# 163 filling products put in front of 23 operations of the attention, by a table

## The chip, the cores and the metric

The kernel runs on one NeuronCore of one Trainium2 chip. Its engines are TensorE (PE, with its weight loads as PEld), VectorE (DVE), ScalarE (ACT), GpSimd (POOL) and SyncE (SP, which issues DMAs). The metric is the device time of one execution in microseconds; lower is better. Before the change three runs took 992.38, 987.22 and 990.80 us, so the median is 990.8 us.

## The reference

Three layers are computed one after the other. The first is a recurrent attention over 768 steps, for 4 batches and 8 heads of width 40:

```
y[t]  = r[t] . state
Sa    = state . a[t]
state = state * w[t] - outer(Sa, b[t]) + outer(v[t], k[t])
```

The second is a gated MLP on x of 4 x 768 x 320: `h = relu(x @ w_in)`, its second half is normalised and mixed along the sequence by `w_spatial`, and the gated product goes through `w_out`. The third sends every token to one of 8 experts (`relu(x @ w1[e]) @ w2[e]`, scaled by the expert's probability). All three give fp32.

## The kernel before, in words

The attention takes the first 480 us or so and is the only part that the diff touches. The 768 steps are cut into 12 chunks of 64, so that 4 batches give 48 units, numbered q = 0 to 47 in the order of the work; one unit is all 8 heads of one batch and chunk, as 4 pairs of heads. A unit passes through named operations, each a handful of instructions on one engine:

- Preparation, long ahead of use: `loadE` (DMA), `stF` (scans of the decay, DVE), `stK` and `stB` (DVE or POOL), `stQ` (PE, line 280), `stT` (PE, line 298), `stL`, `stLk`, `stKT` (ACT, out of PSUM).
- Inverses of small triangular blocks: groups of units go out to DRAM, are inverted by long rows of small DVE operations (`pm`/`psb` or `cm`/`cs`) and come back by DMA; then for two units at a time `gA`, `pA`, `c1`, `c2` on PE (lines 366, 376 and 379, 391, 399), with copies on DVE and ACT between them.
- The chain from unit to unit: `s` (line 434), `z` (443, with 415 for the next unit), `w` (452, 453), `t` (462) and `y` (470, 471) on PE, with `sc`, `zc`, `wc` on ACT and `tc`, `yc` on DVE between them.

The order of all these on each engine is written out before the program runs, by the function `plan`: a list of operations with durations and due times, run through a small model. Where the model sees PE without work it puts in a filling product: `heat(bank)` multiplies a 128x128 tile of zeros (`hz`) by a 128x256 tile of zeros into a PSUM bank that nobody uses just then (line 229), and the result is never read. A `tied` filling product (line 239) does the same with one operand that DVE has just written, so that it can't run before that DVE operation. A PSUM bank is one of five tiles (`pk`, `pw`, `pq`, `pvr`, `pc`); `takes` says which operation starts to use a bank, `gives` which one reads it out last. A filling product that comes first on a bank gets a new tile there, and waits for the bank's last reader.

The list that `plan` returns is written into the program one by one, by the loop at the end of `attention`; each engine runs its own instructions in that order. In the program a filling product is two instructions, a weight load and a product. An fp32 product of the attention is four in the trace (two weight loads, two products), a transpose (`stT`) two.

## Time and profile before

| | |
|---|---|
| runs, us | 992.38, 987.22, 990.80 (median 990.8) |
| profiled execution, us | 995.05 |
| its span, first to last instruction, us | 993.5 |
| mean granted TensorE clock | 0.938 |
| PE busy, us (share) | 928.7 (93%), 14053 products |
| PE weight loads busy | 820.3 (83%) |
| DVE busy | 687.4 (69%) |
| ACT busy | 549.8 (55%) |
| POOL busy | 385.2 (39%) |
| filling products (line 229) | 607, in the attention alone |

Times in the profile count from the span's start. A busy PE is not a PE at its peak: products overlap, and their ends are modelled. [...] "issue" as the releaser of a wait means that the profile shows nothing that the engine waited for.

### The profile page before, as it was taken

The numbers are of one execution on the slowest core, as the hardware profiler recorded it, in microseconds if no ns is written. First come the engines' busy times: TensorE is split into PE (matmuls) and PEld (weight loads), VectorE is DVE, ScalarE is ACT, GpSimd is POOL, SyncE is SP. The second block draws the span as 40 slices with busy tenths as digits, with TensorE's granted clock in tenths as the row PEclk, the third lists the DMA queues.
The fourth block names the chain that finished last, engine by engine and source line by source line (L and its number), as shares of the span: only waits on it lengthen the run. The fifth ranks groups of instructions, "written<-read, shape, count | busy, mean of one in ns | idle before, by whom it ended". The sixth has DMA issues, their size and how long they took to land. (4 is left out here: it accounts for less than half of the span.)

```text
span 993.5 us, 33733 instructions
## 1 busy us (share of the span) xinstructions
PE 928.7 (93%) x14053; PEld 820.3 (83%) x14053; DVE 687.4 (69%) x1614; ACT 549.8 (55%) x1251; POOL 385.2 (39%) x560
## 2 busy tenths in 40 slices
PE   8879989999899998899899999999999999999995
PEld 6657767787787776787789999999878999999994
DVE  6666779888669888764676464654675777787782
ACT  7766543766546774466344433434343767667671
POOL 6544733745216541452243025050136443333431
PEclk9687997999869999679899999999999999999998
DMA  6665761757615865245320030210147656444640
GB/s 160 169 165 136 166 154 50 190 127 187 164 45 128 214 156 113 67 113 131 112 61 1 10 89 1 56 42 1 50 166 270 257 209 248 167 161 160 266 158 16
DMA packets 172415, 127.52 MB, mean 128 GB/s; under 512 B 127502, under 2 KB 161168, under 8 KB 170593
## 3 DMA queue, kind: packets, MB, share of 16 engines
q1 hardware_dynamic: 166704, 78.06, 30.9%
q0 software_dynamic: 5552, 47.25, 12.6%
q8 instruction: 112, 1.84, 0.8%
q14 instruction: 47, 0.38, 0.1%
HBM read 108.13 MB, written 26.61 MB: 136 GB/s over the span
## 5 line engine op out<-in xcount | busy, mean ns | idle before, releaser
L1242 DVE TENSOR_TENSOR eWL<-raw,eWH 128x1024 fp32r<-128x1024 f32 (+1 forms) x64 | 86.2, 1356 | 21.2 <-ACT eWH L1240 19.9
L1240 ACT CAST eWH<-raw 128x1024 fp32r<-128x1024 f32 (+1 forms) x85 | 94.4, 1140 | 2.2 <-DMA raw<-in_wt_dram,wid 2.2
L1369 POOL DMA_INDIRECT out_dram<-yo,sid x29 | 39.2, 1352 | 111.7 <-ACT yo L1368 44.9
L229 PEld LDWEIGHTS <-hz 128*128 128x128 bf16 x607 | 56.9, 106 | 27.7 <-issue 11.8
L1279 PE MATMUL e_ph<-xh,eWH 128*128 128x256 f32 x288 | 77.9, 284 | 0.0
L294 POOL TENSOR_SCALAR_AFFINE_SELECT lq<-lq 64x256 f32<-64x256 f32 x96 | 47.0, 489 | 78.1 <-ACT lq L290 70.0
L1279 PE MATMUL e_ph<-xl,eWH 128*128 128x256 f32 x288 | 77.0, 280 | 0.0
L1279 PE MATMUL e_py<-eWH,hh 128*128 128x320 f32 x232 | 73.0, 315 | 0.0
L1279 PE MATMUL e_py<-eWH,hl 128*128 128x320 f32 x232 | 72.3, 312 | 0.2 <-DVE hl L1352 0.2
L1279 PE MATMUL e_py<-eWL,hh 128*128 128x320 f32 x232 | 71.5, 308 | 0.0
L936 PE MATMUL pv<-sh,g_vh 128*128 128x384 f32 x192 | 66.4, 346 | 1.3 <-ACT pv L926 1.2
L936 PE MATMUL pv<-sh,g_vl 128*128 128x384 f32 x192 | 64.9, 338 | 1.1 <-POOL g_vl L916 0.6
L273 POOL TENSOR_TENSOR lq<-etile,GP 64x256 f32<-64x256 f32 (+1 forms) x60 | 46.8, 780 | 46.3 <-DVE GP L262 28.5
L936 PE MATMUL pv<-sl,g_vh 128*128 128x384 f32 x192 | 64.6, 336 | 0.0
L426 POOL TENSOR_SCALAR_AFFINE_SELECT X<-X 64x256 f32<-64x256 f32 x48 | 23.2, 483 | 97.3 <-ACT X L422 81.2
L1326 DVE SCALAR_TENSOR_TENSOR hl<-e_ph,hh 128x256 fp32r<-128x256 f32 x96 | 37.9, 418 | 26.3 <-ACT hh L1325 23.3
L470 PE MATMUL py<-X,kt 128*40 128x104 f32 x384 | 51.4, 269 | 4.6 <-DVE X L465 4.3
L465 DVE TENSOR_TENSOR X<-pw,ut 64x416 f32<-64x416 f32 x48 | 27.8, 578 | 40.4 <-PE pw L462 28.8
L1279 PEld LDWEIGHTS e_ph<-xh,eWH 128*128 128x128 f32 x288 | 54.4, 189 | 0.9 <-ACT xh L1269 0.2
L1279 PEld LDWEIGHTS e_ph<-xl,eWH 128*128 128x128 f32 x288 | 54.3, 188 | 0.1
L1325 ACT ACTIVATE hh<-e_ph 128x256 fp32r<-128x256 f32 x96 | 36.5, 384 | 31.0 <-PE e_ph L1279 25.9
L1279 PE MATMUL e_ph<-xh,eWL 128*128 128x256 f32 x192 | 53.6, 279 | 0.0
(363 smaller groups left out, 3159.8 us busy)
## 6 DMA issues: line engine op xcount, KB each, us to landing
etile<-in_ed_dram SPq DMA_DIRECT2D x96, 161.2 KB
DT<-in_dd_dram SPq DMA_DIRECT2D x96, 80.0 KB
pu<-BP SPq DMA_DIRECT2D x48, 128.0 KB
yT<-yt SPq DMA_DIRECT2D x48, 104.0 KB
X<-in_vd_dram SPq DMA_DIRECT2D x96, 50.0 KB
groom<-in_w_dram SPq DMA_DIRECT2D x20, 192.0 KB
xs<-xr SPq DMA_DIRECT2D x3, 1176.0 KB
praw<-in_win_dram SPq DMA_DIRECT2D x6, 512.0 KB
```

The lines of the kernel that those rows point to most:

```text
L229: nc.tensor.matmul(out=hcur[bank],lhsT=hz[:,0:128],rhs=hz,start=True,stop=True)
L273: eng.tensor_tensor(out=LQ[q][r,sl],in0=ar[r],in1=GP[q%NBIG][r,:,0:64],op=ALU.mult)
L294: nc.gpsimd.affine_select(out=LQ[q][r,h],in_=LQ[q][r,h],pattern=[[0,NP],[1,64]],**sel)
L465: nc.vector.tensor_tensor(out=x[0:64,:,0,:],in0=pw[0:64],in1=ut[0:64].unsqueeze(1).to_broadcast([64,NP,104]),op=ALU.mult)
L470: nc.tensor.matmul(out=py[0:40,p,:],lhsT=KT[q][:,p,0:40],rhs=x[:,p,0,:],start=False,**acc)
L936: for j,(l,r) in enumerate(t): nc.tensor.matmul(out=pv,lhsT=l,rhs=r,start=False,stop=j==len(t)-1,skip_group_check=True)
L1240: nc.scalar.copy(WH[:,c0:c1],raw[:,c0:c1])
L1242: else: V.tensor_tensor(out=WL[:,lc(c0):lc(c1)],in0=raw[:,c0:c1],in1=WH[:,c0:c1].bitcast(F32),op=ALU.subtract)
L1279: for i,(l,r) in enumerate(t): nc.tensor.matmul(out=out,lhsT=l,rhs=r,start=i==0,stop=i==len(t)-1)
L1325: nc.scalar.activation(hh[:,j],ph,AF.Relu)
L1326: V.scalar_tensor_tensor(out=hl[:,j],in0=ph,scalar=0.0,in1=hh[:,j].bitcast(F32),op0=ALU.max,op1=ALU.subtract)
L1369: nc.gpsimd.indirect_dma_start(out=out,out_offset=IO(ap=self.sid[:,h,s:s+1],axis=0),in_=yo[:,h],in_offset=None,bounds_check=B*S-1,oob_is_e ...
```

## The change

A table `HEATS` names 23 operations and a count for each, 163 in all. When the loop that writes the planned list into the program comes to one of them, it first writes that many filling products, one after the other, into the first bank of a list `rest`. That list holds the banks which no operation uses at that place of the list; a bank leaves it when an operation takes it, and goes to its end when the operation that reads it out last has been written. So its first member has been free for the longest. `plan` itself knows nothing of the table: the order of all other instructions is as it was, on every engine.

```diff
+HEATS={('s', 2):8,('z', 0):14,('stQ', 5):18,('stQ', 7):6,('stT', 8):3,('stT', 9):5,('stQ', 9):7,('gA', 4):4,('c1', 4):7,('pA', 6):3,('stT', 22):5,('pA', 8):12,('s', 12):3,('stQ', 28):3,('s', 13):9,('y', 15):4,('c1', 20):3,('pA', 22):14,('pA', 36):6,('c1', 36):6,('pA', 38):11,('pA', 42):8,('y', 46):4}
 def plan(ops,K,late,cols,takes,gives):
...
+    rest=["pk","pw","pq","pvr","pc"]
     with tc.manual_schedule():
         for t_,_,n,e in out:
             o=ops.get(n)
             if n[0]=="heat": heat(n[1]); continue
             if n[0]=="tied": tied(n[1],n[2]); continue
-            for k in takes.get(n[0],()): hcur.pop(k,None)
+            if n in HEATS:
+                for _ in range(HEATS[n]): heat(rest[0])
+            for k in takes.get(n[0],()):
+                hcur.pop(k,None)
+                if k in rest: rest.remove(k)
+            if n[0] in gives and gives[n[0]] not in rest: rest.append(gives[n[0]])
```

The table's rows tell a reader little without their places, so here are two of them on PE. The lines below the table are numbered one higher after the change (line 229 becomes 230, and so on). The first place is `pA` of the units 22 and 23, behind `y` of unit 19; in the names `XT` is the inverse, `GA` a tile that DVE wrote just before, `hz` the zeros. Before:

```order
L470 MATMUL py<-X_144,kt 40x104
L471 MATMUL py<-X_144,kt 40x104
L376 MATMUL pc<-XT_146,GA 32x32 x4
L379 MATMUL pc<-GA,XT_146 32x16 x2
L376 MATMUL pc<-XT_146,GA 32x32 x4
```

Between `y` and `pA` stood nothing. After:

```order
L471 MATMUL py<-X_144,kt 40x104
L472 MATMUL py<-X_144,kt 40x104
L230 LDWEIGHTS hz
L230 MATMUL pq<-hz 128x256
...
L230 LDWEIGHTS hz
L230 MATMUL pq<-hz 128x256
L377 MATMUL pc<-XT_146,GA 32x32 x4
L380 MATMUL pc<-GA,XT_146 32x16 x2
L377 MATMUL pc<-XT_146,GA 32x32 x4
```

Fourteen pairs of weight load and product have come in front of `pA` (two of them are shown), on the bank `pq`. Nothing else moved. The second place is `stQ` of unit 28, behind a transpose `stT`; `pq` and `pvr` are its two output banks, `kb` and `lq` its operands. Before:

```order
L399 MATMUL pc<-XT_145,GT_122 32x32 x16
L462 MATMUL pw<-Wt,XT_146 64x104 x8
L298 MATMUL pk<-ident,kb 128x104 x4
L280 MATMUL pq<-lq,kb 64x64 x2
L280 MATMUL pvr<-lq,kb 64x64 x2
```

After:

```order
L463 MATMUL pw<-Wt,XT_146 64x104 x8
L299 MATMUL pk<-ident,kb 128x104 x4
L230 LDWEIGHTS hz
L230 MATMUL pq<-hz 128x256
L230 LDWEIGHTS hz
L230 MATMUL pq<-hz 128x256
L230 LDWEIGHTS hz
L230 MATMUL pq<-hz 128x256
L281 MATMUL pq<-lq,kb 64x64 x2
L281 MATMUL pvr<-lq,kb 64x64 x2
```

Three filling products came in between, on the bank that `stQ` itself takes next; the tile is given up to it.

## Rows read from the trace of the kernel before

**Rows 1.** Windows of three stages; busy us (count) by engine, granted clock, DMA.
```profile
core 0: us, PE busy (x) PEld busy (x) DVE busy (x) ACT busy (x) POOL busy (x), PEclk, DMA share, GB/s
20.00:86.00 66.00, 55.13 (x1043) 41.72 (x1042) 40.85 (x104) 41.77 (x126) 29.80 (x48) 0.74 0.60 161
85.00:476.00 391.00, 363.88 (x9685) 302.52 (x9681) 301.77 (x719) 228.84 (x579) 168.68 (x274) 0.91 0.56 134
476.00:994.00 518.00, 494.58 (x3223) 465.58 (x3223) 332.02 (x756) 263.06 (x505) 171.96 (x212) 0.98 0.33 119
```

**Rows 2.** The page, span and granted clock in 40 slices.
```profile
span 993.5 us, 33733 instructions
PEclk9687997999869999679899999999999999999998
```

**Rows 3.** Windows of stretches at half clock, and one at full.
```profile
149.60:163.30 13.70, 13.70 (x270) 11.10 (x261) 12.70 (x32) 4.97 (x14) 1.20 (x3) 0.50 0.08 21
197.50:200.80 3.30, 3.30 (x52) 2.55 (x51) 2.24 (x2) 0.70 (x2) 1.53 (x3) 0.50 0.90 178
265.70:293.00 27.30, 27.06 (x594) 23.56 (x595) 13.48 (x34) 11.99 (x33) 3.60 (x8) 0.50 0.18 46
398.80:412.50 13.70, 13.70 (x289) 11.82 (x287) 8.03 (x21) 6.54 (x17) 3.77 (x6) 0.50 0.17 42
419.30:432.90 13.60, 13.60 (x327) 12.21 (x327) 9.29 (x25) 7.06 (x14) 2.73 (x5) 0.50 0.41 100
300.00:398.00 98.00, 90.14 (x2528) 74.38 (x2526) 83.28 (x205) 61.25 (x152) 45.01 (x76) 1.00 0.66 154
```

**Rows 4.** Who PE waited for, 85 to 476 us: total, times, longest.
```profile
PE pc L376 <- issue: 7.2, 5, 2.6
PE py L470 <- DVE X L465: 4.3, 4, 2.0
PE pc L391 <- issue: 2.3, 3, 0.8
```

**Rows 5.** Timeline of PE, five waits; in brackets the idle time before.
```profile
149.19 0.18 PE L376 MATMUL pc<-XT,GA 32*32 32x32 f32 x1 [1.40 <-issue]
...
265.94 0.27 PE L376 MATMUL pc<-XT,GA 32*32 32x32 f32 x3 [2.60 <-issue]
...
385.69 0.23 PE L376 MATMUL pc<-XT,GA 32*32 32x32 f32 x4 [1.08 <-issue]
...
397.65 0.22 PE L376 MATMUL pc<-XT,GA 32*32 32x32 f32 x3 [1.57 <-issue]
...
417.87 0.37 PE L470 MATMUL py<-X,kt 128*40 128x104 f32 x2 [2.02 <-DVE X L465]
```

**Rows 6.** Windows from block end to block end; counts of products and weight loads in brackets.
```profile
137.89:140.63 2.74, 2.73 (x127) 2.46 (x126) 2.60 (x8) 1.95 (x7) 1.34 (x2) 1.00 0.70 169
385.68:388.53 2.85, 2.84 (x126) 2.55 (x126) 2.58 (x7) 1.62 (x5) 0.00 (x0) 1.00 0.23 56
145.73:147.60 1.87, 1.87 (x131) 1.70 (x128) 1.80 (x7) 0.28 (x1) 0.00 (x0) 1.00 0.41 79
381.81:384.43 2.62, 2.62 (x149) 2.31 (x138) 2.52 (x8) 1.21 (x3) 0.00 (x0) 1.00 0.77 214
278.47:281.69 3.22, 3.22 (x144) 2.93 (x140) 2.30 (x6) 0.84 (x2) 0.00 (x0) 0.50 0.02 5
```

**Rows 7.** DMA queue, kind: packets, MB, share of 16 engines; whole run.
```profile
q8 instruction: 112, 1.84, 0.8%
```

**Rows 8.** Timeline of PE, early filling products, and waits at 13.65 and 43.34 us.
```profile
5.67 1.89 PE L229 MATMUL pvr<-hz 128*128 128x256 bf16 x8
...
10.55 1.14 PE L229 MATMUL pvr<-hz 128*128 128x256 bf16 x9
13.65 0.29 PE L415 MATMUL pvr<-DT 40*64 40x64 f32 x2 [1.96 <-DMA DT<-in_dd_dram]
...
43.34 0.18 PE L239 MATMUL pc<-GP,hz 104*128 104x32 bf16 x1 [2.25 <-DVE GP L262]
```

## The prediction

> **What bounds the kernel now.** I read the three stages first. From 85 to 476 us PE is busy 363.88 of 391 us and its granted clock is 0.91; before that it is 0.74; behind 476 us, where the change puts nothing, PE is busy 495 of 518 us at 0.98 [rows 1]. So the last stage only moves as a whole: what the attention gains or loses, the kernel gains or loses. The page shows where the clock is low: in slices 2 to 4, 7, 11 to 12 and 17 to 18 of 40 above all [rows 2]. [...]

> Then I compared such stretches with one at full clock. From 300 to 398 us the clock is 1.00 and the fullest engine beside PE is DVE, 83.28 of 98 us or 85%. From 265.7 to 293 us, at 0.50, PE is busy 27.06 of 27.3 us and DVE 13.48, only 49%. From 398.8 to 412.5 us it is 13.70 and 8.03 (59%). There PE alone sets the pace, and it does so since its clock is halved. From 149.6 to 163.3 us PE is full too, but DVE has 12.70 of 13.7 us [rows 3]: there a faster PE would meet a full DVE.

> What PE did just before a fall: it waited. The idle times of 1.40 us up to 149.19, 2.60 up to 265.94 and 1.57 up to 397.65 each have a stretch at 0.50 at their end or within two microseconds of it; the one of 1.08 us up to 385.69 has none. The stretch from 419.3 follows 2.02 us in which `y` waited for DVE [rows 3, 5]. In the waits of `pA` the releaser is "issue": no semaphore explains them.

> [...]

> **The change part by part.** It adds 163 products and 163 weight loads, takes nothing away and moves nothing else. Filling products took 1.89/8 = 0.24 us apiece from 5.67 us on and 1.14/9 = 0.127 from 10.55 on, the tail of the last one included [rows 8]: half pace, then full pace. 163 at full pace are 163 x 0.127 = 20.7 us of PE, the far end of their cost.

> Most of that lies in waits that PE has anyway. The counts fit them: 14 fills (1.8 us) ahead of `pA` of unit 22, inside which 2.60 are waited; 12 (1.5) where 1.40 is waited; 11 (1.4) for 1.57; 6 (0.8) for 1.08 [rows 5]; 18 (2.3) ahead of the 2.25 us up to 43.34; the 8 and 14 of the first units ahead of 1.96 us of waiting for a DMA [rows 8] and of the copies of the next units. No such wait stands behind `stQ` 7 and 28, `s` 13, `y` 15 and `pA` 42: 6+3+9+4+8 = 30 fills, 3.8 us. That is the upper end of what is uncovered; the lower end is nothing, since PE has slack where DVE sets the pace. I take the 12 fills of `y` 15 and `pA` 42, which stand in or near the chain from unit to unit: 1.5 us.

> The bank costs nothing: the first of `rest` has been read out longest ago, and the operation that takes it next stands on PE itself. If one did wait for the last reader once, the nearest price is a wait of `y` for DVE, 4.3/4 = 1.1 us [rows 4]; I take nothing.

> The gain is in the clock. A wait filled with products is no idle time, and filling products do hold the clock up: from 5.67 to 10.55 us PE ran little but them and small products of `s`, and their pace went from 0.24 to 0.127 us apiece [rows 8]. So I expect no fall behind a wait that is filled for the most part. What a stretch at full clock would take lies between two ends: half its PE time, or its DVE time at the 85% of rows 3.
> - 265.7 to 293: saves 27.06/2 = 13.5 by PE, 27.3-13.48/0.85 = 11.4 by DVE.
> - 398.8 to 412.5: 6.9 by PE, 13.7-8.03/0.85 = 4.3 by DVE.
> - 149.6 to 163.3: 6.9 by PE, nothing by DVE (12.70/0.85 is over 13.7).
> - 197.5 to 200.8: 1.7 by PE, 3.3-2.24/0.85 = 0.7 by DVE.

> I take the DVE end, since in the full-clock stretch DVE is nearest to its limit. Together 16.4 us; the PE end is 29.0. The stretch at 419.3 stays: no fill stands ahead of `y` of unit 38. For 20 to 86 us I take nothing, for the first inverses wait there for DVE and DMA; the far end is 66 x (1-0.74) = 17 us, all of it as if PE set the pace [rows 1].

> One correction. Each fill is two instructions, so the block ends move forward among the operations. The fills up to `pA` 22 sum to 128, which is 256 instructions, exactly one block: from there to `pA` 36 every block ends at the same instruction as before. One such end stands in `pA` 24, and the block up to it took 3.22 us at half clock [rows 6]; at full clock it is one of about half that, 1.6 us, like the one of 1.87 that was followed by 1.40 us of waiting and a fall. No fill stands there. So I expect the clock to hold past 266 us and to fall again about half way, near 280 us of the old time, and count half of the 11.4: 5.7 us.

> Sum: 5.7+4.3+0.7+0 = 10.7 us gained, 1.5 lost, net 9.2. The profiled execution took 995.05 us (its span of 993.5 and 1.55 around it), 0.4% over the median of 990.8, so it would take 985.9, and the median becomes 981.6, say 982 us.

> **The rivals.**
> - *The clock stays up everywhere behind a fill, and PE sets the pace* (963 us). All four stretches give their PE end: 990.8-29.0+1.5 = 963.3. For it: PE is full in each [rows 3]. Against it: DVE at 93% in the first, and the unfilled block end in `pA` 24. A version in between has DVE's pace and no new fall at `pA` 24: 990.8-16.4+1.5 = 975.9. It is what follows if block ends cost nothing of their own. [...]
> - *The waits only move* (990 us). The shifted block ends strike dense places without a fill, the clock falls there instead, and only the last stretch, 4.3 us, is gained against 3.8 us of uncovered fills. For it: the ends do shift by 2 to 256 instructions from the start to unit 22. Against it: by count of the instructions, the ends nearest to the old waits now fall in `gA`, `stQ` and `z` rather than in the middle of `pA` 8 and 22, and blocks with fills are longer ones.
> - *Slower: the fills become plain work* (1004 us). The place is 120 to 470 us, with 163-61 = 102 fills, 13.0 us. If block ends move away from the fills, the wait comes elsewhere in full, the fill is paid in full, and no stretch is shortened: 990.8+13.0. It decides as soon as more than the gain of 10.7 us is uncovered. For it: the table's places are those of waits in this trace, which the table itself shifts. Against it: from unit 23 to 36 the shift is one whole block, and behind it at most 2 x 23 = 46 instructions (to `pA` 42).

> **How the numbers follow.** Chances: forecast with its own range of 974 to 986 us 0.46; clock up everywhere (960 to 976) 0.20; waits only move (986 to 996) 0.20; slower 0.14. About 0.5%, 5 us, is what a measurement here can tell from no change. So faster is 0.66, same 0.20, slower 0.14. The range is 963 to 997: it leaves out the best of the second case and most of the last.

> **What would show it.** In the profile after: the granted clock 1.00 from 149 to 163 and from 398 to 412 us or where these units then lie; a stretch at 0.50 that begins near `pA` 24 instead of `pA` 22; DVE over 80% where the clock is full; "issue" waits of PE whose sum is not above before. The forecast is wrong at its base if the clock falls right behind filled waits, or if it stays up and the units take no less time; wrong in one term if the fall at `pA` 24 does not come.

## The result, and the profile after

The changed kernel takes 998.35 us (median of 21 executions), the kernel before 988.39 beside it: ratio 1.0122, 95% interval [1.0098, 1.0146]. It is slower by 1.2%, which the interval tells from no change, and outside the range of 963 to 997. The profiled execution took 996.88 us. (Ratios here leave disturbed executions out; medians and the other columns of the table of runs below do not, which changes no value there called "above the line" by more than 0.7 us.)

The same three windows after the change (the last ends 2 us later), columns as in [rows 1]:

```profile
20.00:86.00 66.00, 56.19 (x1243) 43.74 (x1235) 45.70 (x115) 46.41 (x142) 31.97 (x51) 0.92 0.64 163
85.00:476.00 391.00, 364.56 (x9620) 300.87 (x9611) 297.94 (x709) 225.53 (x570) 169.55 (x274) 0.93 0.55 133
476.00:996.00 520.00, 496.34 (x3223) 467.70 (x3223) 338.20 (x756) 263.55 (x505) 168.52 (x212) 0.98 0.34 119
```

The granted clock (a share of full speed) rose as it should: 0.74 to 0.92 in the first stage, 0.91 to 0.93 in the second, and over the whole run 0.938 to 0.956 in these two executions. The kernel became slower all the same. So the first question is not where the clock went, but what was paid for it.

The granted clock in 40 slices, to be held against [rows 2]:

```profile
span 995.3 us, 34059 instructions
PEclk9989978999779999989999999999997999999998
```

Whom PE waited for between 85 and 476 us (total, times, longest; lines are one higher than in [rows 4]):

```profile
PE pc L392 <- issue: 2.9, 2, 2.7
PE pc L377 <- issue: 2.8, 4, 1.5
...
PE pvr L281 <- issue: 1.4, 1, 1.4
```

The waits of `pA` without a releaser fell from 7.2 to 2.8 us, but others came up in `c1` (L392, 2.3 to 2.9, now one long one) and in `stQ` (L281). Their places, on PE's timeline (start, length, in brackets the idle time before):

```profile
136.18 0.37 PE L281 MATMUL pvr<-lq,kb 40*64 40x64 f32 x1 [1.45 <-issue]
...
256.78 0.47 PE L392 MATMUL pc<-T,BP 32*32 32x32 f32 x17 [2.69 <-issue]
...
285.44 0.23 PE L377 MATMUL pc<-XT,GA 32*32 32x32 f32 x4 [1.50 <-issue]
```

These are `stQ` 21, `c1` 20 and `pA` 24, 5890 and 1533 recorded instructions of PE apart (semaphore instructions counted), that is 23 and 6 blocks of 256 within 3, and each with a fall of the clock to 0.50. In the windows of the stretches the falls read so (the last is the old place of one that is gone):

```profile
136.10:152.90 16.80, 16.66 (x306) 13.32 (x306) 8.43 (x25) 6.25 (x16) 2.49 (x6) 0.50 0.31 79
258.80:272.50 13.70, 13.62 (x237) 11.06 (x236) 6.94 (x20) 5.92 (x15) 4.17 (x8) 0.50 0.64 145
286.10:296.40 10.30, 10.30 (x180) 9.12 (x178) 4.89 (x12) 4.62 (x13) 0.82 (x2) 0.50 0.08 20
398.80:412.50 13.70, 12.18 (x471) 10.28 (x471) 10.85 (x28) 7.62 (x20) 5.67 (x6) 1.00 0.22 49
```

Unit by unit, from the start of the first product of `y` of one unit to that of the next one named (us, read from the timelines; "again" is a second profiled execution of the unchanged kernel, and `e11` one of a run below whose attention is the unchanged one):

| from, to | before | again | `e11` | after |
|---|---|---|---|---|
| start, `y` 0 | 86.0 | 83.0 | 80.3 | 80.8 |
| `y` 0, `y` 4 | 49.7 | 48.9 | 50.3 | 51.2 |
| `y` 4, `y` 6 | 29.1 | 30.5 | 29.6 | 35.4 |
| `y` 6, `y` 15 | 70.5 | 70.6 | 81.4 | 69.5 |
| `y` 15, `y` 19 | 26.2 | 27.1 | 27.7 | 32.8 |
| `y` 19, `y` 22 | 39.4 | 37.4 | 34.1 | 34.5 |
| `y` 22, `y` 35 | 91.0 | 90.1 | 90.6 | 90.4 |
| `y` 35, `y` 47 | 80.3 | 77.6 | 77.0 | 75.6 |
| `y` 47, end (the tail) | 521.4 | 521.4 | 521.8 | 525.1 |

Against the first profile, what was won in one place stands beside what was lost in the next: 4.9 us in units 19 to 22, and 6.6 lost in units 15 to 19, where the new wait in `c1` 20 is. But the three executions of the unchanged attention differ among themselves, and only three differences lie outside their spread by more than 1.5 us, all of them losses (the largest gain is 1.4 us, in units 35 to 47): units 4 to 6 (behind the wait in `stQ` 21), units 15 to 19, and the tail, in which nothing was changed and which is 3.7 us longer. The first two are clear by little: in `e5` below, whose blocks end as in the kernel before, these units take 33.1 and 30.7 us.

The rise of the clock is also not where the losses are. Summed from the stretches in the traces, the time at half clock up to `y` 0 is 34 us before, 27 again and 10 after; from `y` 0 to `y` 47 it is 72, 61 and 55; in the tail 18, 17 and 23.

The tail was the surprise. In its waits one line is new. Before, in its place, PE waited for `xg` from a DMA and not for `xl` (first the kernel before, then the changed one):

```profile
PE e_px L1266 <- DMA xg<-xs,gid: 2.4, 1, 2.4
...
PE e_ph L1286 <- DVE xl L1277: 4.9, 1, 4.9
```

With both waits the granted clock falls to half, and with the longer one for longer: from 750.40 to 753.80 us before, from 750.40 to 760.60 after.

```profile
750.40:753.80 3.40, 3.40 (x14) 2.08 (x13) 1.11 (x2) 0.96 (x2) 3.37 (x2) 0.50 0.90 287
...
750.40:760.60 10.20, 8.71 (x41) 8.72 (x42) 3.18 (x11) 1.53 (x4) 4.03 (x6) 0.50 0.45 156
```

Here is the place on the timeline, first in the second execution of the kernel before:

```profile
740.09 1.22 POOL L1257 DMA_INDIRECT xg<-xs,gid  x1 [6.21 <-DVE wid L1198]
...
741.33 0.18 DVE L1207 TENSOR_TENSOR se<-se,hs 128x20 f32<-128x20 f32 x1
...
743.91 5.77 POOL L1242 TENSOR_TENSOR eWL<-raw,eWH 128x1280 fp32r<-128x1280 f32 x2
744.62 0.56 DVE L1270 TENSOR_TENSOR xl<-e_px,xh 128x384 fp32r<-128x384 f32 x1 [2.65 <-ACT xh L1269]
```

and in the changed kernel:

```profile
740.86 1.22 POOL L1264 DMA_INDIRECT xg<-xs,gid  x1 [4.16 <-DVE eWH L1248]
...
744.05 6.40 DVE L1214 TENSOR_TENSOR se<-se,hs 128x20 f32<-128x20 f32 x1
744.68 5.72 POOL L1249 TENSOR_TENSOR eWL<-raw,eWH 128x1280 fp32r<-128x1280 f32 x2
...
750.82 1.01 DVE L1277 TENSOR_TENSOR xl<-e_px,xh 128x384 fp32r<-128x384 f32 x2
751.88 0.58 PE L1286 MATMUL e_ph<-xl,eWH 128*128 128x256 f32 x1 [4.90 <-DVE xl L1277]
```

A product of 20 columns on DVE, 0.18 us elsewhere, takes 6.40 and ends with POOL's long subtraction of two pieces (`eWL`; POOL's starts are rough). Before, POOL waited 6.21 us ahead of its gather and came to its long pieces 2.4 us behind `se`; after, it waited only 4.16. Its gather reads `xs`, which has to be written first. (The releasers in brackets are DVE instructions; that the gather waits for the write is inferred from the distances below.) The DMA traffic, from the issue of that write on, in 40 slices of 0.165 us, of the second execution of before and of after:

```profile
DMA  0000049999999999999999897100000000000000
GB/s 0 0 0 0 0 162 352 371 390 380 380 380 380 380 371 380 380 285 361 380 470 390 314 409 276 57 0 0 10 10 10 10 19 19 29 19 29 0 0 0
...
q8 instruction: 1, 0.02, 1.3%
```

```profile
DMA  0000049999999999996999999600000000000000
GB/s 0 0 0 0 0 143 361 399 361 409 352 409 352 390 371 399 352 352 209 342 361 409 352 399 352 228 0 0 0 0 0 0 0 0 0 0 0 0 0 0
```

In the kernel before one block of instructions (the one packet on q8) is fetched amid this write, and packets of the write come through singly until 6.2 us after the issue. In the changed kernel no fetch falls there, and it is done at 4.3. In both, POOL's gather starts 1.4 to 1.5 us behind the last packet (740.09 and 740.86). So the kernel before was kept from the collision of DVE and POOL by a late write, and that by the place of a block end. The profiles of all runs below bear this out: in the five whose blocks end as in the kernel before a fetch starts 3.4 to 3.5 us behind the issue and the write ends at 5.8 to 6.2; in the nine with shifted blocks no fetch starts before 4.3 us, and the write ends at 4.3 to 4.4.

### The profile page after: what moved, and what is told of

Read it like the earlier page. It is cut to its first block, busy times and chain, and to the rows that moved or that the text cites. A ratio compares the mean times of both kernels' runs of the same rounds, so it can differ in the third digit from the quotient of the medians.

```text
span 995.3 us, 34059 instructions
## 1 busy us (share of the span) xinstructions
PE 933.6 (94%) x14216; PEld 824.4 (83%) x14216; DVE 694.3 (70%) x1614; ACT 549.9 (55%) x1251; POOL 383.2 (38%) x560
## 3 DMA queue, kind: packets, MB, share of 16 engines
q8 instruction: 114, 1.87, 0.8%
## 5 line engine op out<-in xcount | busy, mean ns | idle before, releaser
L230 PEld LDWEIGHTS <-hz 128*128 128x128 bf16 x770 | 70.9, 103 | 28.3 <-issue 11.1
L1376 POOL DMA_INDIRECT out_dram<-yo,sid x29 | 37.1, 1280 | 114.0 <-ACT yo L1375 54.4
```

The source lines that it names most:

```text
L230: nc.tensor.matmul(out=hcur[bank],lhsT=hz[:,0:128],rhs=hz,start=True,stop=True)
L1376: nc.gpsimd.indirect_dma_start(out=out,out_offset=IO(ap=self.sid[:,h,s:s+1],axis=0),in_=yo[:,h],in_offset=None,bounds_check=B*S-1,oob_is_e ...
```

## The experiments

Theory C: what counts is where the ends of PE's blocks of 256 instructions fall, and the 326 added instructions move them, in the tail too (326 = 256 + 70). Rivals: the fills cost their own time on PE (L); the number of instructions costs (D). In the expectations of the first four runs L is still called A, B says that only the clock differs, and D of `e4_late` says that the fills are paid in full wherever they stand.

One measure for all: the clock differs from execution to execution, so each time is also compared at equal clock. Let h be the time at half clock, 2 x (1 - mean granted clock) x 985 us. Over 104 executions of the kernel before, the time is 953.3 + 0.324 h us, with 1.9 us of scatter. "Above the line" is the mean, over all executions of a kernel, of its time minus this value: the cost that is not the clock's. It is an estimate: the line is that of the kernel before, and that a microsecond at half clock costs the same in the other kernels, whose clock falls at other places, is assumed. The tail is read from one profiled execution of each kernel.

| kernel | median us | ratio and interval | h, us | above the line | tail, us |
|---|---|---|---|---|---|
| before, 104 executions | 984 to 990 | 1 | 105 | 0 | 521.4 |
| after (all 163 fills) | 998.35 | 1.0122 [1.0098, 1.0146] | 85 | 18.4 | 525.1 |
| `e1_before_again` | 987.91 | 1.0006 [0.9956, 1.0056] | 105 | -0.4 | 521.4 |
| `e2_thin` | 1000.98 | 1.0152 [1.0098, 1.0206] | 128 | 6.7 | 525.2 |
| `e3_early` | 1004.08 | 1.0220 [1.0165, 1.0275] | 122 | 12.5 | 525.3 |
| `e4_late` | 993.01 | 1.0103 [1.0063, 1.0142] | 88 | 11.8 | 526.9 |
| `e5_pad256` | 984.42 | 0.9961 [0.9917, 1.0005] | 98 | -0.1 | 518.2 |
| `e6_pad70` | 997.78 | 1.0067 [1.0007, 1.0126] | 113 | 6.9 | 526.2 |
| `e7_tail_order` | 990.56 | 1.0038 [0.9998, 1.0078] | 78 | 12.1 | 518.3 |
| `e8_early_aligned` | 986.18 | 1.0008 [0.9963, 1.0053] | 91 | 4.6 | 517.4 |
| `e9_pad_late_order` | 984.95 | 1.0036 [0.9994, 1.0079] | 99 | 0.8 | 517.3 |
| `e10_late_order` | 987.18 | 1.0041 [1.0005, 1.0077] | 100 | 0.1 | 518.0 |
| `e11_order_only` | 989.22 | 1.0034 [0.9994, 1.0075] | 101 | 2.0 | 521.8 |
| `e12_thin_order` | 994.19 | 1.0055 [1.0020, 1.0091] | 116 | 3.0 | 517.5 |

**The kernel before once more** (no edit), for the scatter.

> The kernel before, unchanged, for the granted clock and the time of several executions. The profiled execution of before (995.05 us) stands 6.7 us over its median of 988.39, so it may not be typical. Theory A (the fills cost PE time, the clock gives part back): over executions, time and mean clock lie on one line, and this line lies below that of the changed kernel (which ran from 991 us at 0.965 to 1005 at 0.945) by some 10 to 15 us at equal clock. Theory B (only the clock differs, the fills cost nothing): both kernels lie on the same line, and before simply has a higher clock in most executions than the 0.938 of the profile. Ratio 1.000 by both.

Same time. The changed kernel does not lie on the line of these executions but 18.4 us above it, so B falls; A had forecast 10 to 15. The profile, though, has no stretch at half clock from 398.8 us on; its clock falls once, at 409.5, and units 35 to 38 take 22.1 us without any fill, where the first profile had 26.1. One of my four stretches was a matter of the execution.

**Thin fills**: same places, same instructions, 8 columns instead of 256.

```diff
-            for _ in range(HEATS[n]): heat(rest[0])
+            for _ in range(HEATS[n]): heat(rest[0],8)
```

> The 163 fills stand at the same places as 163 products of 8 columns instead of 256: as many instructions, so every block of 256 instructions ends where it does after the change, but next to no PE time and next to no activity. Theory A (PE time of the fills): most of the loss goes, ratio to before 0.998 to 1.005. Theory C (the shifted block ends make new waits in dense places, which cost time and clock whatever the fills are): still slower, ratio 1.010 to 1.020, with the fetch waits at stQ of unit 21, pA of 20, c1 of 20 and pA of 24 as after the change.

As slow as the full ones, so the change is slow without the fills' length. But not for the same reason: h is 128 and not 85, and the cost beside the clock is 6.7 and not 18.4 us. By the line, the full fills buy 42 us at full clock, 13.7 us of time, and pay 11.7 for it. A thin one takes 0.04 us, a full one 0.125:

```profile
6.12 0.34 PE L230 MATMUL pk<-hz 128*128 128x8 bf16 x8
```

```profile
397.87 1.37 PE L230 MATMUL pk<-hz 128*128 128x256 bf16 x11
```

That is (0.34/8 and 1.37/11, the end of a group's last one included) 163 x (0.125 - 0.04) = 13.9 us more if nothing hides them; 11.7 were paid.

**Half of the table each**: the 61 fills up to `stQ` 9, and the other 102.

```diff
-HEATS={('s', 2):8,...,('stQ', 9):7,('gA', 4):4,...,('y', 46):4}
+HEATS={('s', 2):8,...,('stQ', 9):7}          # e3_early
+HEATS={('gA', 4):4,...,('y', 46):4}          # e4_late
```

> Only the 61 fills up to stQ of unit 9 (before 65 us). In the profile after, y of unit 0 came at 80.8 instead of 86.0 us and that of unit 4 at 132.0 instead of 135.7. Theory A: these fills lie in waits, so the gain of 4 to 5 us at unit 0 is kept: ratio 0.993 to 1.000. Theory C: the block ends of all that follows are shifted by 122 instructions and new waits take it back: 1.000 to 1.010.

> Only the 102 fills from gA of unit 4 on, in the places of the waits that the trace of before shows there, with block ends at first where they are before (shift 0 up to unit 4, then 8 to 134 instructions). Theory A: the 13 us of fills are mostly covered by waits up to unit 8 and from unit 36 on; ratio 0.995 to 1.005. Theory D (the fills are paid in full wherever they stand, since PE is full between block ends): ratio 1.008 to 1.013, that is 102/163 or more of the loss.

Both slower than before; 61 fills alone are worse than all 163, and outside both ranges that were expected for them. The 102 fills come out in the range of "paid in full" (1.008 to 1.013) and not in that of "mostly covered". The two losses do not add up to that of the whole table, and both kernels have the long tail, as every one whose blocks are shifted there and that has no copy (below). For the tail the number of fills does not matter: what matters is that there is a shift.

**Shift alone.** Thin products in waits of PE ahead of 63 us: 128 of them (256 instructions, so that every block ends where it did) or 35 (70 instructions).

```diff
-HEATS={('s', 2):8,...,('y', 46):4}
+HEATS={}
+PADS={('s',0):10,('s',1):10,('vr',0):56,('stT',8):12,('stT',9):18,('stQ',9):22}   # e5_pad256
+PADS={('vr',0):35}                                                                # e6_pad70
+            for _ in range(PADS.get(n,0)): heat(rest[0],8)
```

> The kernel before with 128 thin products (8 columns each, 256 instructions with their weight loads) put into waits of TensorE before 63 us, and none of the 163 fills. Theory C (what counts is where the ends of the blocks of 256 TensorE instructions fall): every end behind 63 us stands at the same instruction as in the kernel before, so the ratio is 1.000 within 0.005, the attention from the first product of unit 0 on takes what it takes there (unit 4 to unit 6 30 us, not 34), the tail behind unit 47 takes 521.4 us and not 525, and VectorE's se<-se,hs takes 0.18 us. Theory D (more instructions on TensorE's queue cost time whatever their number, some 12 us for 326 by the thin fills): 256 more cost about 8 to 10 us, ratio 1.008 to 1.010.

> The kernel before with 35 thin products (70 instructions) in one wait of TensorE at 12.7 us: behind it the block ends stand 70 instructions earlier in the program, as behind the last of the 163 fills (326 = 256 + 70). Theory C: the tail behind unit 47 takes 525 us with the 6.4 us of VectorE's se<-se,hs in it (+3.7), the attention is shifted too and by the block times of the trace has more short blocks than unshifted (waits below 3.3 us of block time 16.5 against 13.3 us): ratio 1.005 to 1.015. Theory D (the number of instructions): 70 of them cost 2 to 3 us, ratio 1.002 to 1.003, and the tail stays at 521.4.

256 added instructions cost nothing that the interval shows, 70 cost 0.7%. This is theory C against D, and D falls: the larger number is the cheaper one. (The thin products stand at other places in the two kernels, too; for the tail that makes no difference, but what the shift does in the attention is not read from this pair.) The tail's small product, by the view of the tile `se` (times in ns), first with 256, then with 70:

```profile
L1216 DVE TENSOR_TENSOR se<-se,hs x1: 179/179/179, 748.5 to 748.5; 128x20 f32<-128x20 f32 x1
```

```profile
L1216 DVE TENSOR_TENSOR se<-se,hs x1: 6410/6410/6410, 732.7 to 732.7; 128x20 f32<-128x20 f32 x1
```

And the fetch is back amid the write of `xs` with 256 (first), and absent with 70, in the same 40 slices from the issue on:

```profile
DMA  0000049999999999996899899510000000000000
...
q8 instruction: 1, 0.02, 0.9%
```

```profile
DMA  0000049999999999997699999700000000000000
```

Two misses: units 4 to 6 were to take 30 us and took 33.1, and the aligned tail was to take 521.4 us and took 518.2. For the tail the traces show a difference in the clock. In the kernel before PE runs at half clock behind its wait for `xg` (above) and here:

```profile
477.40:484.00 6.60, 5.21 (x12) 4.13 (x13) 1.03 (x3) 0.60 (x1) 0.35 (x2) 0.50 0.53 160
```

With the 256 instructions the granted clock is 1.00 in both places, and in the whole tail it is 0.50 only near 510.2 to 513.5 us and in the last 7 to 10 us, where every profile has it. That is 6.8 us less at half clock for 3.2 us less time. The same order holds over all profiles: with the end left out, tails of 517.3 to 518.3 us have 3.4 us at half clock, those of 521.4 to 521.8 have 10.2, and the longer ones 13.7 to 17.1. Why the clock falls there in one aligned kernel and not in the other is open.

**Early fills with the shift taken out**: the 61 of `e3_early` and 67 thin ones.

```diff
+HEATS={('s', 2):8,...,('stQ', 9):7}
+PADS={('s',0):8,('s',1):8,('vr',0):36,('stT',8):5,('stT',9):6,('stQ',9):4}
```

> The first 61 fills alone (which gave 1.022) with 67 thin products in waits before 63 us beside them: together 256 instructions, so that behind unit 0 every block end stands as in the kernel before. Theory C: the loss of the 61 fills was the shift behind them and not their own time; it goes, and what the early clock gives stays: ratio 0.996 to 1.001, tail 521.4 us, unit 4 to unit 6 30 us. If the fills themselves or the number of instructions cost the time: 1.015 to 1.025, as without the thin products.

More instructions than in `e3_early`, and 1.0008 instead of 1.0220. The loss of `e3_early` was the shift behind it: the wait in the tail, and 31 us more at half clock. What is left, 4.6 us above the line where the 128 thin products of `e5_pad256` have -0.1, is of the size of 61 x (0.125 - 0.04) = 5.2 us of fills. The tail is short here as well: 517.4 us and not the 521.4 expected.

**The tail's collision taken out** of the changed kernel: POOL first copies one word of `eo`, the last of DVE's short chain.

```diff
                 weights(1)
+                gate=self.wp.tile([128,1],F32,name="gate",bufs=1)
+                nc.gpsimd.tensor_copy(gate,self.eo[:,0,0:1])
                 for i in (3,4): self.split(0,i,nc.gpsimd)
```

> The changed kernel, with a copy of one word of eo by GpSimd ahead of the two pieces of eWL at the start of the experts, so that they begin behind VectorE's short chain. If the 4.9 us wait of TensorE for xl is VectorE's se<-se,hs held up by GpSimd's long eWL (6.40 us beside it, 0.18 us without): se takes 0.18 to 0.23 us, TensorE's wait for xl is below 1 us, the tail behind unit 47 goes from 525 to 520 or 521 us, and the time is 4 to 5 us under that of the changed kernel (993 to 995, ratio 1.005 to 1.008). If the wait only moves to what GpSimd does later: tail 524 to 525, ratio 1.012.

As the first theory said, and further than it said (tail 518.3 us and not 520 to 521, time 990.6 and not 993 to 995):

```profile
751.41 0.18 DVE L1214 TENSOR_TENSOR se<-se,hs 128x20 f32<-128x20 f32 x1
...
752.11 0.18 POOL L1311 COPY gate<-eo 128x1 f32<-128x1 f32 x1
752.26 5.81 POOL L1249 TENSOR_TENSOR eWL<-raw,eWH 128x1280 fp32r<-128x1280 f32 x2
...
754.64 0.38 PE L1286 MATMUL e_ph<-xl,eWH 128*128 128x256 f32 x1 [0.20 <-DVE xl L1277]
```

The tail is 6.8 us shorter, and the kernel 6.3 us nearer to the line. That is the price of the collision: the wait of 4.9 us and the 10.2 us at half clock behind it are both gone. It is more than the tail's share of the loss against the kernel before. That kernel has a wait of 2.4 us of its own there, which the change takes away, and its tail is only 3.7 us shorter than that of the changed kernel: a third of the 12.1 us that are lost in all (below).

**The copy alone, and two attempts at a better kernel**: the copy in the kernel before (`e11_order_only`); the copy with the 35 fills from `pA` 36 on (`e10_late_order`); the same with the 128 thin products (`e9_pad_late_order`).

> The kernel before with GpSimd's copy of one word of eo alone. In the kernel before GpSimd's long eWL starts 2 us behind VectorE's se<-se,hs anyhow, so by the theory of the overlap nothing is held up and the copy changes nothing: ratio 1.000 within 0.004, tail 521 us. If the copy does more than keep the two apart (or the tail's gain in the changed kernel had another cause): tail 517 to 518 us here too, ratio 0.996.

> The 35 fills from unit pA 36 on and GpSimd's copy, without the thin products. Theory C: nothing moves up to unit 35; units 35 to 47 75 to 76 us, 2 to 4 less than before; tail 518 to 521 us with no wait of TensorE for xl above 1 us: ratio 0.993 to 0.998. If fills are paid at their own length: 0.998 to 1.001. Without the copy this kernel's tail, shifted by 70 instructions, would lose 4 to 5 us.

> Three things together: the 128 thin products before 63 us (256 instructions, which gave 0.996), the 35 fills of the table from unit pA 36 on, and GpSimd's copy of one word of eo ahead of its long pieces. Theory C: up to unit 35 the block ends stand as in the kernel before, from there to unit 47 as in the changed kernel (there the units 35 to 47 take 75.6 us, against 77.6 and 80.3 of two executions before), and the tail, now shifted by 70 instructions, is kept from the 4.9 us wait by the copy (518 us instead of 525): ratio 0.990 to 0.995. If fills are paid at their own length (35 x 0.107 = 3.7 us): 0.996 to 1.000.

In the kernel before the copy wins nothing, as no collision is there to take out (tail 521.8). The other two have the short tail (518.0, 517.3) and stand on the line, but their ratios are 1.004: none of my versions beats the kernel before beyond its interval. Of the expectation for them the tail came true and the ratio did not, under either theory; from unit 35 to 47 they take 77.2 us each, no better than the 77.6 of the second execution of before. With a tail 3.4 and 4.1 us shorter they should be faster. 35 fills at 0.125 us are 4.4 us, which would take that back; that they do is not shown.

**Length alone**: thin fills with the copy, to be held against `e7_tail_order`.

> The 163 products at their places but of 8 columns, with GpSimd's copy of one word of eo. Over the executions of the kernel before, the time is 953.7 us and 0.32 us for each us at half clock. Against this line the 163 fills with the copy stand 12.2 us higher, the 163 thin products without the copy 7.1, the changed kernel 18.5. Theory L (a fill is paid at its own length: 163 x (0.107 - 0.04) = 10.9 us, and the tail's wait 4.9 to 6.3): with both gone it stands 0 to 2 us above the line, and its time follows from its clock alone: with the clock that the thin products had (127.7 us at half clock, 23 to 28 more than before) 8 us more, ratio 1.004 to 1.010. Theory N (the number and the places cost, not the length): 10 to 12 us above the line as with the full fills, ratio 1.015 or more. Tail 517 to 518 us under both.

3.0 above the line where the full fills have 12.1: a little more than the 0 to 2 of theory L, far from the 10 to 12 of N, and the ratio is inside the range of L; N falls. (Up to 2 of the 3.0 us may be the copy's, by `e11_order_only`.) The full fills pay 9.1 us and have 38 us less at half clock, 12.3 us. Each held against the kernel before as it ran beside it, these are 10.1 us, 34 us and 10.9 us. In plain time the full fills are a little faster than the thin ones: the means are 990.6 and 993.8 us with the copy, 999.4 and 1001.5 without. So the split into what is paid and what is gained rests on the line.

## Why the prediction was wrong

The mean time of the changed kernel is 12.1 us over that of the kernel before: 18.4 above the line, less 6.3 by its 19 us less at half clock. Without any line, the copy in the tail alone takes the ratio from 1.0122 to 1.0038, whose interval includes 1. By the steps:

1. **"Most of that lies in waits that PE has anyway": failed, and this is the largest error.** I took 1.5 us uncovered of 20.7. By the line the runs give 9.1 to 10.1 (with the copy) and 11.7 (without), of at most 13.9 that the length adds. The fills were counted against the waits of the old trace, but these waits are block ends, and a table of 326 instructions moves the block ends: at `pA` 8, 22 and 38, where [rows 5] has 1.40, 2.60 and 1.57 us, no wait stands behind the fills any more, so they fill nothing. `pA` 22 and its 14 fills in the changed kernel, with no idle time between them:

```profile
271.21 2.30 PE L230 MATMUL pq<-hz 128*128 128x256 bf16 x14
273.44 0.26 PE L377 MATMUL pc<-XT,GA 32*32 32x32 f32 x8
```

   My text had this as what speaks for the slower rival ("the table's places are those of waits in this trace, which the table itself shifts"), and gave it 0.14.
2. **"The last stage only moves as a whole": failed.** It is 3.7 us longer than before (525.1 against 521.4), and the collision in it costs 6.3 to 6.8 us by the pair with and without the copy. The stage has a transfer and two engines whose order hangs on when one block of PE's instructions is fetched. I counted the shift of the block ends up to 476 us and stopped where the change puts nothing, although the shift goes on to the end.
3. **The gain by the clock, 10.7 us: failed where it was counted.** More than half of it, 5.7 us, was to come from the stretch of 265.7 to 293 us. Units 15 to 22, where that stretch lies, take 67.3 us after; the unchanged attention has 65.6, 64.5 and 61.8. Held against thin products at the same places, the full ones gain 10.9 to 13.7 us by the line; that this is near 10.7 is luck, for it is another quantity than the one forecast. Against the kernel before only 6.3 are left: thin products alone, that is the shift alone, have 4 to 22 us more at half clock than the kernel before as it ran beside them, 1.3 to 7.3 us of time (`e12_thin_order`, `e2_thin`). I had allowed for one new fall, at `pA` 24, and not for those at `stQ` 21 and `c1` 20, with their stretches from 136.1 and 258.8 us on.
4. **That fall came**, at 285.44 us behind 1.50 us of waiting, with the stretch from 286.1 on. Counting blocks worked where I did it. I did it at one place; the same count puts ends into `stQ` 21 and `c1` 20, and there the clock fell as well.
5. **The stretch at 398.8 went, and units 35 to 38 became 3.9 us shorter** (4.3 forecast), with DVE at 10.85 of 13.70 us, 79%. But that this term came true is luck: the unchanged attention did the same in two other executions, 22.1 and 22.0 us. The price of a stretch was taken from a single execution, whose clock of 0.938 lay under the mean of 0.947.
6. **The bank** cost nothing that the waits show. For 20 to 86 us I took nothing, and nothing is shown: `y` 0 comes at 80.8 us, in the unchanged attention at 80.3 to 86.0, although the clock there rose most.

"The waits only move" was right that they move, and missed both the length of the fills and the tail. The slower rival had the right condition, more uncovered than gained: 9 to 12 us against 6.3.

The step that failed first is a rule of reading: a wait without a releaser was treated as a hole at a fixed place of the program. It is a hole at a fixed count of instructions: in the kernel before, the first products behind the waits up to 149.19, 265.94, 385.69 and 397.65 us stand 5888, 5888 and 769 recorded instructions of PE apart, that is 23, 23 and 3 blocks of 256 within one. `e5_pad256` and `e6_pad70` differ in where blocks end, and by 7.0 us above the line, about what their tails differ by (8.0). The largest single wait that a moved block end brought, 4.9 us, comes by way of a DMA, POOL and DVE.

## What to carry to other kernels

Instructions added to an engine that is fed in blocks, as PE is here in blocks of 256, move every block end behind them, to the end of the program: pad to a whole block (256 thin instructions cost nothing here that the interval shows, 70 cost 0.7%), or count again, and only then price what was added. A fill is worth what the clock gives less its own length (by the line 12.3 us against 9.1 here), and it has no cover unless a wait is still behind it after the shift. Before a cost is laid to a change, run its instructions without their work, and its shift without its instructions; and take the clock out of each time by a line through many executions of one kernel.

## What the runs showed of the hardware that was not expected

- A microsecond at half clock costs 0.324 us here, over 104 executions of the kernel before, and not 0.5. That other engines hide the rest is likely, but no run shows it.
- One block fetch of 16 KB amid a write of 1.2 MB held up the end of that write from 4.3 to between 5.8 and 6.2 us behind its issue (five profiles with such a fetch, nine without).
- DVE's product `se<-se,hs` and the subtraction `se<-se` behind it, both of two SBUF operands, take 0.18 us each, but beside POOL's subtraction of 128x1280 in two pieces the product took 6.40 us (after) and 6.41 (`e6_pad70`), the subtraction 6.29 (`e3_early`). `xl`, which reads PSUM, took 0.56 beside it, and 0.54 to 0.56 in all 29 places of the kernel before. Why the one is held up and the other is not, no run shows.
